# New order of TensorE units, new list priorities and new planner durations in a segment-recurrent attention kernel

## The chip, the cores and the metric

The kernel runs on one core of one Trainium2 chip. The metric is the time of one execution on the device in microseconds (us).

## The reference

`A` is a transformer layer with a recurrent memory, `B` a GELU feed-forward network; each has a layernorm ahead of it, and B normalizes once more inside. With 2048 tokens, width 512, 32 heads of 128, 8 memory rows, segments of 32 tokens and a hidden width of 1792:

```
mem = mem0
for s in range(64):
    h = concat([mem, x[32*s : 32*s+32]])            # 8 + 32 rows
    q, k, v = h @ Wq, h @ Wk, h @ Wv                # 32 heads of 128
    p = softmax(where(mask, q @ k.T / sqrt(128), -1e9))
    o = (p @ v) @ Wo
    mem = o[:8]                                     # next segment's memory
    outs.append(o[8:])
h  = x + A(layernorm(x))
h2 = h + B(layernorm(h))     # B(x) = gelu(layernorm(x) @ w1 + b1) @ w2 + b2
```

The segments depend on one another through `mem`: the next segment's projections need this segment's output projection.

## The kernel before, in words

All weights are loaded once into SBUF. For every segment TensorE runs units, most of them four matmuls side by side in the four column groups of the array:

- K0, K1, Q0, Q1, V0, V1: projections of the first and second 16 heads, four passes each (one per 128 rows of the width). `passes` (L796, and L547 where the stationary operand of the unit before is kept) records them. A pass is four matmuls of 512 columns.
- SC0, SC1 (`sc_mm`, L963): scores of the memory rows and of the 8 last tokens; `sc_softmax` follows with a max on VectorE (`nmc`, L972), the exponentials on ScalarE (`EC`, L976), a reciprocal (`rsc`, L979), a product (`PC`, L982) and a transpose (`PTC`, L983) on VectorE.
- PV0, PV1 (`pv_c`, L994 and L998): the product of those probabilities with V. SA (`sa_mm`, L1025) are the scores of the other 24 tokens' rows, whose result no later segment needs; PVA (`pv_a`, L1055, two units) is their product with V, done one segment later. PV and PVA use 32 rows of the array and all its columns (MR in the code); the other units of the loop use all rows and 32 columns (MC).
- WO (`wo_units`, L1083, eight units): the output projection. Then VectorE transposes (`TT`, L1095) and sums halves into `hT` (L1089), the next segment's memory rows.
- F0, F1: work that does not belong to the recurrence. For segments 4b to 4b+2 it is the K, Q or V projection of the last 8 tokens of each of the next four segments (`hB`, eight passes); for segment 4b+3 it is eight passes of `wo_B` (FB, L1112), all counted as F1.

`place(s)` names segments 1 to 3 a1 to a3, 60 to 63 z60 to z63 and the 56 between them m0 to m3 by s mod 4. `ORDERS[place]` is TensorE's order in a segment, written out: "V1.0.2" takes units 0 and 1 of V1. `TURNED[place]` lists the projections whose passes run backwards. Everything on the other engines is placed by a list scheduler (`Sched.schedule`) when the program is built:

```
heapq.heappush(heap, (-o.rank - BONUS.get(o.key, BONUS.get(o.kind, 0.0)), pos[o], o.gidx, o))
```

`rank` is the longest path of planned durations to the end, `BONUS` adds a number in us per kind of result and place (`PTC0@m3`: the PTC of SC0 in a segment of place m3). An operation taken from the heap goes into the first free gap of its engine on the planner's clock, and copies out of PSUM go to VectorE or ScalarE, whichever ends sooner. Each engine's instructions then run in the order of their planned starts, with semaphore waits; engines run their queues in order. The durations (`dur=`), `SWITCH` (a change between MC and MR) and `HOP` (the way from engine to engine) exist only in the planner.

Layernorm of later tokens (`ln1`, L734 to L738) runs in places m1 and later: statistics on VectorE, `rst` with a power on GpSimd (L737), then `xn` on VectorE. `nat` does the same for the attention's output (L1134 to L1137). After segment 63 comes the feed-forward network, whose order on TensorE is fixed in the code, as is `START`, the order of segment 0.

## Time and profile before

| | us |
|---|---|
| median of 3 executions | 805.24 |
| lowest, highest | 804.34, 806.07 |
| profiled execution: span from the first to the last instruction | 802.2 |

The page gives the profiled execution as its span alone; its own time is among those of the first two rows, some 3 us above the span. In the rows of the profile the columns are the start in us from the start of the span, the length in us, engine, line, operation, result and operands, shape and count; a bracket tells the idle time before and what ended it. The rows for TensorE begin where a matmul begins to read, and their ends overlap the next one's start, so the cost of a unit is read from its start to the next start.

### The profile page before, as it was taken

Reading aid. Unit: us, or ns where it says so; the run is one execution under the profiler, and the core shown is the slowest. Engines: PE = TensorE matmul, PEld = TensorE weight load, DVE = VectorE, ACT = ScalarE, POOL = GpSimd, SP = SyncE. Lnnn points to the kernel's source line nnn. Section 1 sums busy time; section 2 is a strip of 40 time slices with the busy share of each in tenths; the row PEclk is TensorE's granted clock in tenths of the full one; section 3 lists DMA queues with packets and bytes.
Section 4 is the critical chain, followed back from the end, with each engine's and each line's share of the span. In section 5 each row is a group of like instructions: output and inputs, shape, how many; then the busy total and the mean of one; then the engine's idle time right before and its main releaser. Section 6 shows DMA issues by size and latency. Waiting matters only on the chain.

```text
span 802.2 us, 46835 instructions
## 1 busy us (share of the span) xinstructions
PE 775.9 (97%) x21699; PEld 423.1 (53%) x20880; DVE 600.7 (75%) x1847; ACT 558.0 (70%) x1580; POOL 90.1 (11%) x211
## 2 busy tenths in 40 slices
...
DMA packets 65555, 48.77 MB, mean 61 GB/s; under 512 B 28996, under 2 KB 63308, under 8 KB 63820
## 3 DMA queue, kind: packets, MB, share of 16 engines
...
q8 instruction: 166, 2.72, 1.4%
q14 instruction: 33, 0.27, 0.1%
q10 hardware_dynamic: 332, 0.27, 0.1%
...
## 4 chain that ended last, share of the span: by engine, by line
PE 91%; DMA 3%; DVE 2%; ACT 1%; SPq 1%; issue 1%; POOL 0%; DVEq 0%; ACTq 0%
PE ps L796 43%; PE ps L1083 15%; PE ps L547 8%; PE quad L1465 6%; PE ps L1451 5%; DMA WQ<-in_A_Wq_dram 3%; PE ps L1112 3%; PE quad L994 3%; PE quad L1055 2%; PE ps L1025 2%; PE ps L1233 1%; PE ps L963 1%; PE quad L963 1%; SPq L708 1%; PE quad L998 1%
## 5 line engine op out<-in xcount | busy, mean ns | idle before, releaser
L1083 PE MATMUL ps<-WO,OT 128*32 128x256 bf16 x4224 | 140.6, 274 | 0.1
L796 PE MATMUL ps<-WQ,hT 128*32 128x512 bf16 x1864 | 131.6, 379 | 0.7 <-DVE hT L1089 0.5
L796 PE MATMUL ps<-WV,hT 128*32 128x512 bf16 x1364 | 125.2, 381 | 0.0
L796 PE MATMUL ps<-WK,hT 128*32 128x512 bf16 x1700 | 123.6, 380 | 0.1
L815 ACT ACTIVATE kq<-ps 128x512 bf16<-128x512 f32 x160 | 95.4, 597 | 32.3 <-PE ps L796 26.4
L1083 PEld LDWEIGHTS ps<-WO,OT 128*32 128x32 bf16 x4224 | 100.9, 96 | 26.5 <-ACT OT L814 5.5
L814 ACT CAST kq<-ps 128x512 bf16<-128x512 f32 x162 | 94.8, 585 | 19.9 <-PE ps L796 13.1
L814 ACT CAST OT<-quad 128x128 bf16<-128x128 f32 x191 | 84.4, 442 | 27.0 <-PE quad L998 18.8
L839 DVE STREAM_TRANSPOSE KALL<-kq 128x256 f32<-128x256 f32 x160 | 71.2, 445 | 15.0 <-ACT kq L814 11.8
L796 PEld LDWEIGHTS ps<-WQ,hT 128*32 128x32 bf16 x1864 | 50.3, 97 | 58.8 <-issue 19.0
L861 POOL COPY ZC<-QTB 128x256 bf16<-128x256 bf16 x64 | 25.6, 401 | 477.2 <-PE ps L963 455.7
L796 PEld LDWEIGHTS ps<-WK,hT 128*32 128x32 bf16 x1700 | 45.8, 96 | 56.9 <-issue 14.5
L547 PE MATMUL ps<-WV,hT 128*32 128x512 bf16 x684 | 67.6, 379 | 0.0
L796 PEld LDWEIGHTS ps<-WV,hT 128*32 128x32 bf16 x1364 | 38.4, 97 | 47.3 <-issue 36.6
L839 DVE STREAM_TRANSPOSE QT<-kq 128x256 f32<-128x256 f32 x128 | 57.0, 445 | 6.5 <-ACT kq L815 1.9
L1454 ACT ACTIVATE WQ<-ps,b1t 128x512 bf16<-128x512 f32 x42 | 28.9, 688 | 46.6 <-PE ps L1451 46.6
L1095 DVE STREAM_TRANSPOSE TT<-ps 128x256 f32<-128x256 f32 x66 | 29.7, 450 | 36.3 <-PE ps L1083 36.1
L814 ACT CAST VS<-ps 128x512 bf16<-128x512 f32 x65 | 38.1, 586 | 26.6 <-PE ps L796 26.5
L814 DVE CAST VS<-ps 128x512 bf16<-128x512 f32 x63 | 41.8, 663 | 5.4 <-PE ps L796 5.4
L1541 DVE TENSOR_TENSOR WV<-quad,WV 128x512 bf16<-128x512 f32 (+1 forms) x16 | 10.5, 672 | 45.6 <-PE quad L1465 45.6
L982 DVE TENSOR_TENSOR PC<-EC,rsc 128x128 bf16<-128x128 f32 x128 | 39.7, 310 | 4.3
L1112 PE MATMUL ps<-WO,OTB 128*32 128x512 bf16 x512 | 42.1, 381 | 0.4 <-issue 0.2
...
## 6 DMA issues: line engine op xcount, KB each, us to landing
...
```

What stands on the lines that cost most here:

```text
L547: return e.add_instruction(mybir.InstMatmult(name="I-%d" % (4000000 + _kept[0]), engine=mybir.EngineType.PE, start_tensor_calc=start, stop ...
L796: ins = e.matmul(o, l, m, start=(k == 0), stop=(k == DC - 1), tile_position=(0, 32 * j), skip_group_check=True)
L814: return {"act": (lambda e: e.copy(out, src), t_act(n, ps_)), "dve": (lambda e: e.tensor_copy(out, src), 0.16 + 1.042e-3 * n * fast)}
L815: return {"act": (lambda e: e.mul(out, src, scale_), t_act(n, ps_)), "dve": (lambda e: e.tensor_scalar(out, src, scale_, None, ALU.mult), ...
L839: S.op("dve", lambda e: e.transpose(out, src), reads=[("kq", i)], writes=[key], dur=t_dve(256) + 0.02, after=after)
L982: S.op("dve", lambda e: e.tensor_tensor(PC[:, r].rearrange("p t a -> p a t"), EC[:, r], bc, ALU.mult), reads=[("EC", r), ("rsc", r)], writ ...
L1083: ins = e.matmul(ps[bank][32 * j:32 * j + 32, 0:256], lhs(slot(h)), wo_cols(h, b), start=(k == 0), stop=(k == 15), tile_position=(0, 32 * ...
L1095: S.op("dve", lambda e: e.transpose(tt.rearrange("p c q t -> p (c q t)"), ps[bank][:, 0:256]), reads=[("ps", bank)], writes=[("TT", par)], ...
L1112: ins = e.matmul(ps[bank][32 * j:32 * j + 32, :], OTB[:, bk % 2, slot(h), :], WO[:, h, :], start=(k == 0), stop=(k == 7), tile_position=(0 ...
L1451: ins = e.matmul(ps[bank][:, 0:SBT], W1[:, cc, fc * P:(fc + 1) * P], hnT_of(k)[:, cc, :], start=(cc == 0), stop=(cc == DC - 1))
L1454: S.op("act", lambda e: e.activation(gT[:, fc, :], ps[bank][:, 0:SBT], ACTF.Gelu_apprx_tanh, bias=b1t[:, fc:fc + 1], scale=1.0), reads=[(" ...
L1465: S.op("pe", lambda e: e.matmul(quad[:, t, :], lhs, W2[:, fc, :], **flags), reads=[("W2", part_of(fc))] + gT_keys(k, fc), writes=[("ps", t ...
```

## The change

Only numbers and strings of the plan change, and one operand pair on GpSimd. `ORDERS` and `TURNED` are new for all eleven places. `BONUS` is new as a whole (several hundred entries; the lines with the entries that the prediction names are shown). `SWITCH` and the planned durations of five kinds of TensorE units change. In `nat` the sum var + 1e-5 becomes var * 1.00001 + 1e-10, in the same instruction. No unit, copy, transfer or buffer is added or removed.

```diff
--- before.py
+++ after.py
-SWITCH = 0.1
+SWITCH = 0.095
...
-         "PTC0@m0": -40, "PTC0@m1": 0, "PTC0@m2": 40, "PTC0@m3": -6.68, "PTC0@z60": 10.07, "PTC0@z61": -2.97, "PTC0@z62": 0.85, "PTC0@z63": 2.87,
...
-         "nmc1@a1": 40, "nmc1@a2": 0, "nmc1@a3": -8.5, "nmc1@m0": 5.59, "nmc1@m1": 10.8, "nmc1@m2": 0, "nmc1@m3": 0, "nmc1@z60": 0,
...
-         "rsc0@m0": -40, "rsc0@m1": -40, "rsc0@m2": -8.83, "rsc0@m3": -40, "rsc0@z60": -10.97, "rsc0@z61": 0.08, "rsc0@z62": -13.33,
...
-         "sma@z63": 5.36, "st": 4.55, "st@a1": -40, "st@a2": 9.73, "st@m1": 1.68, "st2": 7.35, "st2@m0": -5.76, "st2@z60": -3.49, "vd@m2": 3.83,
...
+         "PTC0@m0": 38.35, "PTC0@m1": 43.59, "PTC0@m2": -56.34, "PTC0@m3": 39.21, "PTC0@z60": -37.64, "PTC0@z61": -43.05, "PTC0@z62": -3.43,
...
+         "nmc0@z61": 30.27, "nmc0@z62": -37.98, "nmc0@z63": 0, "nmc1": 1.64, "nmc1@a1": 40, "nmc1@a2": -36.64, "nmc1@a3": 3.86, "nmc1@m0": 34.96,
+         "nmc1@m1": 40, "nmc1@m2": -36.44, "nmc1@m3": -36.44, "nmc1@z60": 46.32, "nmc1@z61": 3.56, "nmc1@z62": -40, "nmc1@z63": -36.44,
...
+         "rsc0@a3": 40, "rsc0@m0": -98.2, "rsc0@m1": -39.55, "rsc0@m2": 31.11, "rsc0@m3": -40, "rsc0@z60": 42.35, "rsc0@z61": -40, "rsc0@z62": -40,
...
+         "sma@z63": -6.26, "st": -43.67, "st2": 38.55, "st2@m0": 39.47, "st2@z60": -6.12, "st@a1": -35.8, "st@a2": -40.62, "st@m1": -35.98,
...
-TURNED = {"a1": "K0 Q1 V0", "a2": "K0 Q0", "a3": "V1", "m0": "F0 F1 Q0 V0", "m1": "K0 K1 Q1 V0", "m2": "F0 K0 K1 V0", "m3": "F1 K0 K1 Q1 V0", "z60": "F1 K0 K1 V0 V1", "z61": "Q0 Q1 V0", "z62": "F1 K0 Q0", "z63": "K0 K1 V0 V1"}
-ORDERS = {"a1": "Q0.0.3 K1.0.1 Q0.3.4 K0.0.2 Q1.0.1 K0.2.4 Q1.1.4 K1.1.4 SC0.0.2 V0.0.3 V1.0.1 V0.3.4 V1.1.2 SC1.0.1 V1.2.4 PVA.0.2 PV0.0.1 F1.0.1 WO.0.2 PV1.0.1 WO.2.8 F1.1.2 SA.0.1 F1.2.4",
-          "a2": "K0.0.1 Q0.0.4 K0.1.4 Q1.0.4 K1.0.4 SC0.0.1 V0.0.4 V1.0.3 SC1.0.1 V1.3.4 PVA.0.2 PV0.0.1 F1.0.2 WO.0.2 PV1.0.1 WO.2.8 SA.0.1 F1.2.4",
-          "a3": "Q0.0.2 K0.0.2 Q0.2.4 K0.2.4 Q1.0.4 K1.0.4 SC0.0.1 V0.0.1 V1.0.1 V0.1.4 V1.1.2 SC1.0.1 PVA.0.2 V1.2.4 PV0.0.1 F1.0.2 WO.0.2 PV1.0.1 WO.2.8 F1.2.4 SA.0.1",
-          "m0": "Q0.0.2 Q1.0.1 Q0.2.4 K0.0.4 Q1.1.4 K1.0.4 SC0.0.1 V0.0.1 V1.0.2 V0.1.2 V1.2.3 V0.2.4 SC1.0.1 V1.3.4 F0.0.1 PVA.0.2 PV0.0.1 F0.1.4 WO.0.2 PV1.0.1 WO.2.8 F1.0.4 SA.0.1",
-          "m1": "K0.0.1 Q0.0.2 K0.1.2 Q0.2.4 K0.2.3 Q1.0.1 K0.3.4 Q1.1.4 K1.0.4 SC0.0.1 V1.0.1 V0.0.2 V1.1.2 V0.2.3 V1.2.3 V0.3.4 SC1.0.1 V1.3.4 F0.0.1 PVA.0.2 PV0.0.1 F0.1.4 WO.0.2 PV1.0.1 WO.2.8 F1.0.3 SA.0.1 F1.3.4",
-          "m2": "K0.0.2 Q0.0.4 K0.2.4 Q1.0.4 K1.0.4 SC0.0.1 V1.0.1 V0.0.2 V1.1.2 V0.2.3 V1.2.3 V0.3.4 SC1.0.1 V1.3.4 F0.0.2 PVA.0.2 PV0.0.1 F0.2.4 WO.0.2 PV1.0.1 WO.2.8 SA.0.1 F1.0.4",
-          "m3": "K0.0.1 Q0.0.2 K0.1.2 Q0.2.4 K0.2.4 Q1.0.4 K1.0.4 SC0.0.1 V1.0.1 V0.0.1 V1.1.2 V0.1.3 V1.2.3 V0.3.4 SC1.0.1 F1.0.1 V1.3.4 PVA.0.2 PV0.0.1 F1.1.5 WO.0.1 PV1.0.1 WO.1.8 F1.5.7 SA.0.1 F1.7.8",
-          "z60": "Q0.0.3 Q1.0.1 Q0.3.4 Q1.1.2 K0.0.4 Q1.2.4 K1.0.4 SC0.0.1 V1.0.1 V0.0.4 V1.1.2 SC1.0.1 V1.2.4 PVA.0.2 PV0.0.1 F0.0.4 WO.0.2 PV1.0.1 WO.2.8 SA.0.1 F1.0.4",
-          "z61": "K0.0.1 Q0.0.4 K0.1.4 Q1.0.4 K1.0.4 SC0.0.1 V0.0.4 V1.0.3 SC1.0.1 V1.3.4 PVA.0.2 PV0.0.1 F0.0.4 WO.0.2 PV1.0.1 WO.2.8 F1.0.4 SA.0.1",
-          "z62": "K0.0.1 Q0.0.4 K0.1.4 Q1.0.4 K1.0.4 SC0.0.1 V0.0.2 V1.0.1 V0.2.4 V1.1.3 SC1.0.1 V1.3.4 PVA.0.2 PV0.0.1 F0.0.4 WO.0.2 PV1.0.1 WO.2.8 SA.0.1 F1.0.4",
-          "z63": "Q0.0.2 K0.0.1 Q0.2.4 K0.1.4 Q1.0.4 K1.0.4 SC0.0.1 V0.0.4 V1.0.3 SC1.0.1 V1.3.4 PVA.0.2 PV0.0.1 F1.0.4 WO.0.2 PV1.0.1 WO.2.4 F1.4.5 WO.4.7 F1.5.6 WO.7.8 F1.6.8 SA.0.1"}
+TURNED = {"a1": "K1 Q0", "a2": "K0 K1 Q0 V0", "a3": "Q1 V1", "m0": "Q0 Q1 V0", "m1": "F0 F1 K0 K1 Q1 V0 V1", "m2": "K1 Q0 V0", "m3": "K0 K1 Q1 V1", "z60": "K0 K1 Q1 V0 V1", "z61": "K0 Q0 Q1", "z62": "K0 K1 Q0 Q1 V0", "z63": "K0 Q0 V1"}
+ORDERS = {"a1": "SC0.0.1 Q0.0.1 K0.0.2 Q0.1.2 K0.2.3 Q0.2.4 K0.3.4 Q1.0.1 K1.0.1 Q1.1.4 K1.1.4 V1.0.1 SC0.1.2 V0.0.2 V1.1.2 V0.2.4 SC1.0.1 PVA.0.1 V1.2.4 PVA.1.2 PV0.0.1 WO.0.2 PV1.0.1 WO.2.8 F1.0.1 SA.0.1 F1.1.4",
+          "a2": "K0.0.1 Q0.0.4 K0.1.4 Q1.0.4 K1.0.4 SC0.0.1 V0.0.1 V1.0.2 V0.1.4 SC1.0.1 V1.2.4 PVA.0.2 PV0.0.1 WO.0.2 PV1.0.1 WO.2.8 F1.0.2 SA.0.1 F1.2.4",
+          "a3": "Q0.0.1 K0.0.1 Q0.1.4 K0.1.4 Q1.0.4 K1.0.4 SC0.0.1 V1.0.2 V0.0.4 SC1.0.1 V1.2.4 PVA.0.2 PV0.0.1 F1.0.1 WO.0.2 PV1.0.1 WO.2.8 F1.1.4 SA.0.1",
+          "m0": "Q0.0.2 Q1.0.1 Q0.2.3 K0.0.1 Q0.3.4 K0.1.4 Q1.1.3 K1.0.1 Q1.3.4 K1.1.4 SC0.0.1 V1.0.1 V0.0.1 V1.1.2 V0.1.3 V1.2.3 V0.3.4 SC1.0.1 F0.0.1 V1.3.4 PVA.0.2 PV0.0.1 F0.1.4 WO.0.2 PV1.0.1 WO.2.8 F1.0.2 SA.0.1 F1.2.4",
+          "m1": "K0.0.1 Q0.0.1 K0.1.2 Q0.1.2 Q1.0.1 Q0.2.4 K0.2.3 K1.0.1 K0.3.4 Q1.1.2 K1.1.2 Q1.2.4 V1.0.1 K1.2.4 SC0.0.1 V1.1.2 V0.0.4 V1.2.3 SC1.0.1 PVA.0.2 V1.3.4 F0.0.2 PV0.0.1 F0.2.4 WO.0.2 PV1.0.1 WO.2.8 SA.0.1 F1.0.4",
+          "m2": "Q0.0.1 K0.0.1 Q0.1.4 K0.1.4 Q1.0.4 K1.0.4 SC0.0.1 V0.0.1 V1.0.1 V0.1.2 V1.1.2 V0.2.3 V1.2.3 V0.3.4 SC1.0.1 F0.0.1 V1.3.4 PVA.0.2 PV0.0.1 F0.1.4 WO.0.2 PV1.0.1 WO.2.8 SA.0.1 F1.0.4",
+          "m3": "Q0.0.1 K0.0.2 Q0.1.2 K0.2.3 Q0.2.4 K0.3.4 Q1.0.3 K1.0.1 Q1.3.4 K1.1.4 SC0.0.1 V1.0.1 V0.0.2 V1.1.2 V0.2.4 V1.2.3 SC1.0.1 V1.3.4 PVA.0.2 PV0.0.1 F1.0.4 WO.0.2 PV1.0.1 WO.2.8 F1.4.6 SA.0.1 F1.6.8",
+          "z60": "Q0.0.4 K0.0.1 Q1.0.1 K0.1.4 Q1.1.2 K1.0.1 Q1.2.4 K1.1.4 SC0.0.1 V1.0.1 V0.0.2 V1.1.2 V0.2.4 V1.2.4 SC1.0.1 F0.0.2 PVA.0.2 PV0.0.1 F0.2.4 WO.0.2 PV1.0.1 WO.2.8 SA.0.1 F1.0.4",
+          "z61": "Q0.0.1 K0.0.4 Q0.1.4 Q1.0.4 K1.0.4 V0.0.1 SC0.0.1 V1.0.1 V0.1.4 V1.1.2 SC1.0.1 V1.2.4 F0.0.1 PVA.0.2 PV0.0.1 F0.1.4 PV1.0.1 WO.0.8 F1.0.4 SA.0.1",
+          "z62": "Q0.0.3 Q1.0.1 K0.0.1 Q0.3.4 K0.1.4 K1.0.1 Q1.1.4 K1.1.4 SC0.0.1 V1.0.2 V0.0.1 V1.2.3 V0.1.3 SC1.0.1 V0.3.4 V1.3.4 PVA.0.1 F0.0.2 PVA.1.2 PV0.0.1 F0.2.4 WO.0.2 PV1.0.1 WO.2.8 SA.0.1 F1.0.4",
+          "z63": "Q0.0.2 K0.0.1 Q0.2.4 K0.1.4 Q1.0.2 K1.0.1 Q1.2.4 K1.1.2 SC0.0.1 K1.2.4 V1.0.1 V0.0.1 V1.1.2 V0.1.3 V1.2.3 V0.3.4 V1.3.4 PVA.0.1 SC1.0.1 PVA.1.2 PV0.0.1 F1.0.2 SA.0.1 F1.2.3 WO.0.3 PV1.0.1 F1.3.4 WO.3.8 F1.4.8"}
...
-                         dur=0.215 * len(parts), mode=MC, ni=4 + 4 * len(parts))
+                         dur=0.2165 * len(parts), mode=MC, ni=4 + 4 * len(parts))
...
-                 writes=[bkey], dur=0.13, mode=MC, ni=32)
+                 writes=[bkey], dur=0.12, mode=MC, ni=32)
...
-            S.op("pe", f, reads=[("VS", s % 3, r), ("PTC", r)] + [("VBD", bk % 2, j) for j in range(4)], writes=QK, dur=0.16, mode=MR, ni=40)
+            S.op("pe", f, reads=[("VS", s % 3, r), ("PTC", r)] + [("VBD", bk % 2, j) for j in range(4)], writes=QK, dur=0.145, mode=MR, ni=40)
...
-            S.op("pe", f, reads=[("QT", 0), ("QT", 1), ("KA", par, 0), ("KA", par, 1)], writes=[("ps", bank)], dur=0.25, mode=MC, ni=64)
+            S.op("pe", f, reads=[("QT", 0), ("QT", 1), ("KA", par, 0), ("KA", par, 1)], writes=[("ps", bank)], dur=0.235, mode=MC, ni=64)
...
-                S.op("pe", f, reads=[("VS", par, half), ("PTA", s % 2)], writes=QK, dur=0.13, mode=MR, ni=32)
+                S.op("pe", f, reads=[("VS", par, half), ("PTA", s % 2)], writes=QK, dur=0.108, mode=MR, ni=32)
...
-            S.op("pool", lambda e: e.tensor_scalar(rs, ag[:, 1:2], 1e-5, None, ALU.add), reads=[("ag2", bk)], writes=[("rs2", bk)], dur=0.2)
+            S.op("pool", lambda e: e.tensor_scalar(rs, ag[:, 1:2], 1.00001, 1e-10, ALU.mult, ALU.add), reads=[("ag2", bk)], writes=[("rs2", bk)], dur=0.2)

```

4 lines of the change are left out of this document (2 added, 2 removed), and 131 rows, old and new, of the table BONUS.

## The prediction

> **What bounds the kernel now.** I read the page first, then the stretch of the segment loop, then TensorE's rows in order of time, and last VectorE's rows at the two places where TensorE waits. From the page (span; busy share of TensorE; chain that ended last, by engine; the queue that carries instructions):
>
> ```profile
> span 802.2 us, 46835 instructions
> ...
> PE 775.9 (97%) x21699; PEld 423.1 (53%) x20880; DVE 600.7 (75%) x1847; ACT 558.0 (70%) x1580; POOL 90.1 (11%) x211
> ...
> q8 instruction: 166, 2.72, 1.4%
> ...
> PE 91%; DMA 3%; DVE 2%; ACT 1%; SPq 1%; issue 1%; POOL 0%; DVEq 0%; ACTq 0%
> ```
>
> TensorE holds 91% of the chain, so only its own order and what it waits for can move the time. The loop, with busy time of PE, PEld, DVE, ACT and POOL, the clock and the DMA share:
>
> ```profile
> 80.00:658.00 578.00, 576.63 (x18329) 319.84 (x17354) 496.94 (x1565) 442.89 (x1314) 47.07 (x119) 1.00 0.14 31
> ```
>
> The clock is full. "Busy" counts overlapping ends, so waits have to be read from starts. First passes of segments 1, 4, 60 and 63, then of 27, 29, 30 and 31:
>
> ```profile
> 49.03 1.02 PE L796 MATMUL ps<-WQ,hT 128*32 128x512 bf16 x12
> ...
> 79.91 0.83 PE L796 MATMUL ps<-WQ,hT 128*32 128x512 bf16 x12 [0.24 <-DVE hT L1089]
> ...
> 658.85 0.83 PE L796 MATMUL ps<-WQ,hT 128*32 128x512 bf16 x12
> ...
> 690.38 0.62 PE L796 MATMUL ps<-WQ,hT 128*32 128x512 bf16 x8
> ```
>
> ```profile
> 318.44 0.40 PE L796 MATMUL ps<-WK,hT 128*32 128x512 bf16 x4
> ...
> 339.16 0.40 PE L796 MATMUL ps<-WK,hT 128*32 128x512 bf16 x4
> ...
> 349.38 0.61 PE L796 MATMUL ps<-WK,hT 128*32 128x512 bf16 x8
> ...
> 359.61 0.40 PE L796 MATMUL ps<-WK,hT 128*32 128x512 bf16 x4
> ```
>
> Segments 4 to 59 are 56 segments, 14 of each place, in 658.85 - 79.91 = 578.94 us. The inside of segment 27 (place m3), from its first score unit to the next segment's first pass, with two rows of segment 28 behind it:
>
> ```profile
> 321.90 0.30 PE L963 MATMUL quad<-KALL,ZC 128*32 128x64 bf16 x16
> ...
> 323.53 0.31 PE L963 MATMUL ps<-KALL,ZC 128*32 128x64 bf16 x16
> 323.65 0.40 PE L1112 MATMUL ps<-WO,OTB 128*32 128x512 bf16 x4
> ...
> 324.20 0.37 PE L1055 MATMUL quad<-PTA,VS 32*128 32x32 bf16 x32
> 324.49 0.27 PE L994 MATMUL quad<-PTC,VS 32*128 32x16 bf16 x16
> ...
> 324.73 1.05 PE L1112 MATMUL ps<-WO,OTB 128*32 128x512 bf16 x16
> 325.60 0.39 PE L1083 MATMUL ps<-WO,OT 128*32 128x256 bf16 x8
> 325.93 0.27 PE L994 MATMUL quad<-PTC,VS 32*128 32x16 bf16 x16
> ...
> 326.17 1.71 PE L1083 MATMUL ps<-WO,OT 128*32 128x256 bf16 x56
> 327.70 0.60 PE L1112 MATMUL ps<-WO,OTB 128*32 128x512 bf16 x8
> 328.14 0.40 PE L1025 MATMUL ps<-KALL,QT 128*32 128x32 bf16 x32
> 328.36 0.41 PE L1112 MATMUL ps<-WO,OTB 128*32 128x512 bf16 x4
> 328.86 1.26 PE L796 MATMUL ps<-WQ,hT 128*32 128x512 bf16 x20
> 329.95 1.04 PE L796 MATMUL ps<-WK,hT 128*32 128x512 bf16 x16
> 330.81 0.82 PE L796 MATMUL ps<-WQ,hT 128*32 128x512 bf16 x12
> ```
>
> Prices from start to start: a pass (329.95 to 330.81, four of them) 0.215; a WO unit (326.17 to 327.70, seven) 0.219; a score unit 0.12; SA 0.22. So segment 27 took 328.86 - 318.44 = 10.42, segment 28 (m0) 10.30, segment 29 (m1) 10.22, segment 30 (m2) 10.23: 41.17 for a clean group of four, 576.4 for 14 groups. The other 2.5 us of the 578.94 are single stalls. Two waits recur. At the tail, FB at 328.36 should last 0.22 and lasts 0.50: TensorE waits 0.28 for the next memory rows. In the middle, PVA to PV0 takes 0.29. VectorE there, and the one large stall:
>
> ```profile
> 323.91 0.29 DVE L972 TENSOR_REDUCE nmc<-ps 128x2 f32<-128x128 f32 x1
> 324.12 0.23 DVE L983 STREAM_TRANSPOSE PTC<-PC 128x64 f32<-128x64 f32 x1
> ...
> 327.56 0.41 DVE L738 TENSOR_SCALAR xn<-xr,agg,rst 128x512 bf16<-128x512 bf16 x1 [1.00 <-POOL rst L737]
> 327.93 0.45 DVE L1095 STREAM_TRANSPOSE TT<-ps 128x256 f32<-128x256 f32 x1
> ```
>
> ```profile
> 159.12 0.19 PE L1055 MATMUL quad<-PTA,VS 32*128 32x32 bf16 x2 [0.67 <-issue]
> ```
>
> **The change, part by part.** The work is the same; counting the order strings gives the same units for every place. The sum is made against the span of 802.2 us; the median of the runs is 805.24, so 3.0 us lie around the span and I leave them.
>
> m3, tail. WO's end at 327.70 to the next segment's start takes 1.16, a fixed chain (TT, the sum, hT). Now 3 FB passes and SA (0.87) cover it; the new order puts 4 FB passes and SA (1.08) there, so 0.21 of wait goes: -0.21 x 14 = -2.9. The pass comes from between SC1 and PVA, so the stretch SC0 to PV0, now 324.49 - 321.90 = 2.59, falls to 2.38 if nothing waits. SC1 to PV1 keeps 2.40 (an FB pass replaced by a WO unit). PV0 waits for PTC, and VectorE runs PTC behind the second score unit's max: swapped, PTC would end 0.21 sooner, which is just enough. The new bonuses set PTC0@m3 from -6.68 to 39.21 and nmc1@m3 from 0 to -36.44, which asks for the swap, but rsc0@m3, two steps ahead of PTC0, stays at -40, level with nmc1. Without the swap PV0 waits 0.21 and the whole gain is gone. I take half: -1.5, ends -2.9 and 0.
>
> m1, one more trip into row tiling. The new order puts a V pass and two F0 passes between PVA and PV0, so the array changes shape six times in place of four. Into row tiling costs 0.11 (325.60 to 325.93 is 0.33 against 0.22). The way out is seen once, in segment 3, which has such a trip, beside a PVA that did not wait (segment 26):
>
> ```profile
> 74.78 0.37 PE L1055 MATMUL quad<-PTA,VS 32*128 32x32 bf16 x32
> 75.08 0.61 PE L796 MATMUL ps<-WV,hT 128*32 128x512 bf16 x8
> ```
>
> ```profile
> 314.19 0.37 PE L1055 MATMUL quad<-PTA,VS 32*128 32x32 bf16 x32
> 314.40 0.30 PE L994 MATMUL quad<-PTC,VS 32*128 32x16 bf16 x16
> ```
>
> PVA then leaves after 0.30 against 0.21, so a trip is 0.20. The wait of 0.08 ahead of PV0 goes with it: +0.12 x 14 = +1.7. Ends: +2.8, if PV0 had not really been waiting, and 0, if VectorE sets m1's length and TensorE only waits less. The page on the chip says the same with no price: the Trainium skill, TensorEngine Tiling (Array Packing), Key Properties, has it that changing the tiling mode drains TensorE. The trace agrees; by that rule alone m1 pays the full +2.8 and the time is 1.1 above my sum, which is counted in rival C too.
>
> m0, tail. SA was last; the new order puts two F1 passes behind it, as m1 had before. Those two places had the same counts and differed by 0.08: -0.07 x 14 = -1.0, ends -1.1 and +1.0.
>
> m2. One F0 pass moves from ahead of PVA to behind PV0, so SC0 to PV0 becomes the 2.59 of m3 with its small wait; the group shows what that costs: +0.03 x 14 = +0.4, ends 0 and +1.0.
>
> Single stalls, 2.5 us. The one at 159.12 waits for no semaphore, in a stream of 16 KB instruction blocks (2.72 MB in 166). A new order moves every block edge. Half of them gone: -1.3; ends -2.5 and +2.5. A page of the Trainium skill, Runtime: NRT & Kernel Launch, section Instruction fetch mechanics, says that crossing such a block is mostly hidden; that one row of 0.67 stands among 166 blocks agrees with mostly. By that rule this term is 0 and the sum 1.3 higher, which is counted in rival C.
>
> Segments 1 to 3 take 79.91 - 49.03 = 30.88 though they lack most F work, so they run on latency. SC1 comes a pass earlier in a2 (0.21), a3 loses a trip (0.20), a1 gains one that its waits cover and has its mask unit moved ahead of the projections, for which I put a pass (0.21): -0.6, ends -0.9 and +0.4. Segments 60 to 62 take 690.38 - 658.85 = 31.53, 0.84 above three clean ones of 10.23; z60 and z61 are evened out, z62 and z63 gain a trip each (+0.4): -0.2, ends -0.8 and +0.8.
>
> One answer, nothing: TURNED only flips the direction of passes whose price is 0.215 either way; SWITCH and the durations feed the planner alone; the second POOL operand sits in the same 16 instructions on an engine 11% busy, read by the FFN long after. START, the FFN's order and the weight queue stay; their evacuations are re-sorted: 0, ends -1 and +1.
>
> Sum: -1.5 + 1.7 - 1.0 + 0.4 - 1.3 - 0.6 - 0.2 = -2.5. Span 799.7, time 802.7.
>
> **Rivals.** B, a larger gain: the swap holds, m1's trip is covered by VectorE's pace, most single stalls go: -2.9 + 0 - 1.0 + 0 - 2.5 - 0.9 - 0.4 = -7.7, 797.5. For it: VectorE is busy 497 of 578 us in the loop, so it can be the one that sets m1. Against it: every term must come out at its good end.
>
> C, the change does not do what it says: PTC0 stays behind nmc1, m1 pays the full trip, stalls only move: 0 + 2.8 - 1.0 + 0.4 + 0 - 0.6 - 0.2 = +1.4, and half of the stalls' term back brings it to about 0: 805.2. For it: -40 on rsc0@m3, and a trip is a shown cost.
>
> D, slower: VectorE's queue runs in order, and at 327.56 it sat 1.00 on POOL's power for xn, then ended just as TT (the head of the tail's chain) could start. The bonus of that statistic, st@m1, falls from 1.68 to -35.98. If the wait slides 0.5 later, TT and the next segment slide with it, once in each of 14 groups: +7.0, 809.7. It decides from 0.3 on (+4.2 against a forecast of -2.5). Against it: xn is needed segments later, so it may slide far past TT and cost nothing.
>
> **How the numbers follow.** 0.2% (1.6 us) is about what a measurement of this kernel can tell from no change. My forecast 802.7 has 0.40, with a range of its own of 800.5 to 805.0: 0.30 of it faster, 0.10 the same. B has 0.20, all faster. C has 0.18: 0.14 the same, 0.04 slower. D has 0.22, all slower. So faster 0.50, same 0.24, slower 0.26. The range 797 to 810 leaves out about half of B below and half of D above, 0.2 together; the ends of single terms, added on one side, would go further than that, to 796 and 815.
>
> **What would show it.** Right: m3 segments near 10.3, with 4 FB passes and SA behind WO and 0.07 of wait; PTC ahead of nmc in m3; PVA to V at 0.30 in m1 and m1 segments near 10.35; m0 near 10.23. Wrong: PVA to PV0 at 0.5 in m3 (no swap); VectorE idle on POOL rst with TT behind it and more than 1.16 from WO's end to the next segment; new rows ended by issue; the first passes of segment 1 or the FFN off by over 1 us, which my sum leaves at 0.

## The result, and the profile after

| us | before | after |
|---|---|---|
| median of 4 executions in the same rounds | 805.65 | 816.61 |
| lowest, highest | 804.34, 806.22 | 814.44, 816.99 |
| profiled execution: time | | 814.44 |
| profiled execution: span | 802.2 | 812.7 |

The changed kernel takes 1.0123 times as long, 95% interval 1.010 to 1.0145. The forecast was 802.7, its range 797 to 810: it is slower, and outside the range. The page of the changed kernel, in the same lines as before:

```profile
span 812.7 us, 46821 instructions
...
PE 782.4 (96%) x21699; PEld 419.0 (52%) x20761; DVE 581.7 (72%) x1789; ACT 576.6 (71%) x1638; POOL 87.3 (11%) x211
...
q8 instruction: 166, 2.72, 1.4%
...
PE 93%; DMA 3%; DVE 1%; SPq 1%; ACT 1%; issue 1%; DVEq 0%
```

TensorE has the same 21699 matmuls. VectorE has 58 instructions fewer (1847 to 1789) and ScalarE 58 more (1580 to 1638): copies out of PSUM have changed engine. The prediction had no term for that in the loop. First passes of segments 4 and 60 after:

```profile
81.27 1.05 PE L796 MATMUL ps<-WQ,hT 128*32 128x512 bf16 x16
...
668.69 0.84 PE L796 MATMUL ps<-WQ,hT 128*32 128x512 bf16 x12
```

Segments 4 to 59 take 587.42 instead of 578.94: +8.5 of the 10.5 us. From the other first passes (segment 1 at 50.89, segment 63 at 700.45): the start +1.9, segments 1 to 3 -0.5, segments 60 to 62 +0.2, the rest +0.4. By place, from first pass to first pass, 14 segments each:

| us | before: median, mean | after: median, mean |
|---|---|---|
| m0 | 10.295, 10.299 | 10.290, 10.659 |
| m1 | 10.251, 10.293 | 10.478, 10.525 |
| m2 | 10.221, 10.222 | 10.303, 10.303 |
| m3 | 10.425, 10.539 | 10.409, 10.471 |

The medians give -0.1, +3.2, +1.1 and -0.2, in sum +4.0; what single segments lie above them was 2.2 us before (the prediction, from a clean group, had 2.5) and is 6.7 after. The waits of TensorE between 80 and 690 us (engine, tile, line, what was waited for: total us, times, longest), first before, then after:

```profile
PE quad L1055 <- issue: 0.7, 1, 0.7
PE ps L796 <- DVE hT L1089: 0.2, 1, 0.2
PE ps L1112 <- issue: 0.2, 1, 0.2
```

```profile
PE quad L994 <- DVE PTC L983: 3.1, 1, 3.1
PE quad L994 <- issue: 1.7, 2, 1.0
PE ps L1112 <- issue: 0.8, 3, 0.5
```

So there are three causes: one wait of 3.1 us for a PTC, stalls for instructions (2.5 us in place of 0.9), and a longer median in m1 and m2. The long wait is in segment 52 (m0). The rows of VectorE and PE there, in order of time:

```profile
587.34 0.37 DVE L1224 TENSOR_SCALAR xn<-xT,agg,rst 128x512 bf16<-128x512 bf16 x1
587.63 0.16 DVE L979 RECIPROCAL rsc<-smc 128x2 f32<-128x2 f32 x1
...
589.60 0.24 DVE L983 STREAM_TRANSPOSE PTC<-PC 128x64 f32<-128x64 f32 x1
...
590.39 0.68 DVE L1120 TENSOR_TENSOR oBn<-OTB 32x512 bf16<-32x512 f32 x1
591.10 0.30 DVE L982 TENSOR_TENSOR PC<-EC,rsc 128x128 bf16<-128x128 f32 x1
591.44 0.24 DVE L983 STREAM_TRANSPOSE PTC<-PC 128x64 f32<-128x64 f32 x1
591.74 0.26 PE L994 MATMUL quad<-PTC,VS 32*128 32x16 bf16 x16 [3.08 <-DVE PTC L983]
```

The reciprocal for SC0 is there at 587.63, behind an `xn` of the feed-forward network's layernorm. The planner then put the product and transpose that PV0 needs behind those of SC1 (589.60) and behind `oBn`: 591.44. VectorE is idle for 0.21 us only in this stretch (ahead of the second max, at 588.00); it does other work first. The `xn` puts the reciprocal 0.33 us later than it could be, and on the planner's clock the product for PV0 then no longer fits into the gap ahead of the second max, so the plan has it behind all the others. That is how 0.3 us becomes a wait of 3.1.

### The profile page after: what moved, and what is told of

Its sections match the earlier page's. It is cut to its first block, busy times and chain, and to the rows that moved or that the text cites. A ratio compares the mean times of both kernels' runs of the same rounds, so it can differ in the third digit from the quotient of the medians.

```text
span 812.7 us, 46821 instructions
## 1 busy us (share of the span) xinstructions
PE 782.4 (96%) x21699; PEld 419.0 (52%) x20761; DVE 581.7 (72%) x1789; ACT 576.6 (71%) x1638; POOL 87.3 (11%) x211
## 4 chain that ended last, share of the span: by engine, by line
PE 93%; DMA 3%; DVE 1%; SPq 1%; ACT 1%; issue 1%; DVEq 0%
PE ps L796 43%; PE ps L1083 15%; PE ps L547 8%; PE quad L1465 6%; PE ps L1451 5%; PE ps L1112 4%; DMA WQ<-in_A_Wq_dram 3%; PE quad L994 3%; PE quad L1055 2%; PE ps L1025 2%; PE ps L1233 2%; PE ps L963 2%; PE quad L963 1%; SPq L708 1%; PE quad L998 1%
## 5 line engine op out<-in xcount | busy, mean ns | idle before, releaser
L796 PE MATMUL ps<-WK,hT 128*32 128x512 bf16 x1868 | 143.5, 380 | 0.0
L796 PE MATMUL ps<-WV,hT 128*32 128x512 bf16 x1496 | 125.3, 379 | 0.0
L796 PE MATMUL ps<-WQ,hT 128*32 128x512 bf16 x1584 | 125.1, 385 | 0.2
L814 ACT CAST OT<-quad 128x128 bf16<-128x128 f32 (+1 forms) x192 | 85.2, 444 | 30.5 <-PE quad L998 24.1
L796 PEld LDWEIGHTS ps<-WK,hT 128*32 128x32 bf16 x1868 | 52.7, 97 | 64.4 <-issue 13.8
L796 PEld LDWEIGHTS ps<-WQ,hT 128*32 128x32 bf16 x1584 | 43.4, 97 | 66.5 <-issue 23.4
L796 PEld LDWEIGHTS ps<-WV,hT 128*32 128x32 bf16 x1496 | 43.4, 96 | 40.3 <-issue 23.5
L839 DVE STREAM_TRANSPOSE QT<-kq 128x256 f32<-128x256 f32 x128 | 55.2, 431 | 7.8 <-ACT kq L815 3.1
L547 PE MATMUL ps<-WV,hT 128*32 128x512 bf16 x552 | 55.2, 379 | 0.0
L814 ACT CAST VS<-ps 128x512 bf16<-128x512 f32 x79 | 46.3, 586 | 9.6 <-PE ps L796 8.9
L547 PE MATMUL ps<-WQ,hT 128*32 128x512 bf16 x464 | 46.0, 379 | 0.0
L976 ACT ACTIVATE EC<-ps,nmc 128x64 f32<-128x64 f32 x130 | 39.7, 310 | 4.1 <-DVE nmc L972 3.7
```

The costliest lines, as they stand in the source:

```text
L547: return e.add_instruction(mybir.InstMatmult(name="I-%d" % (4000000 + _kept[0]), engine=mybir.EngineType.PE, start_tensor_calc=start, stop ...
L796: ins = e.matmul(o, l, m, start=(k == 0), stop=(k == DC - 1), tile_position=(0, 32 * j), skip_group_check=True)
L814: return {"act": (lambda e: e.copy(out, src), t_act(n, ps_)), "dve": (lambda e: e.tensor_copy(out, src), 0.16 + 1.042e-3 * n * fast)}
L839: S.op("dve", lambda e: e.transpose(out, src), reads=[("kq", i)], writes=[key], dur=t_dve(256) + 0.02, after=after)
L976: ins = e.activation(EC[:, r, sl, :], o[:, 64 * sl:64 * sl + 64], ACTF.Exp, bias=nmc[:, r, sl:sl + 1], accum_out=smc[:, r, sl:sl + 1])
```

## The experiments

Ratios are to the kernel before, run on the same chip. LOCK is a constant of the kernel that pads TensorE's stream with empty instructions at the third unit of each m0, so that a block of 256 instructions ends at a chosen place; both kernels had 106:

```
if LOCK is not None and o.tag is not None and units == SKIP + 1 and seg % 4 == 0 and seg:
    owed = (LOCK - at) % FETCH_N
```

"Margin" is the last number in the rule by which a TensorE unit with several semaphore waits hands the earlier ones to units ahead of it:

```
if c.start < p.start + p.dur + self.lat(p, o) + 0.1:
    break
```

**1. Segment 52's `xn` (r_hn).** The changed kernel, with `hn0`, the early `xn` of L1224, given a lower priority in m0.

```diff
+BONUS = {"hn0@m0": -40, ...
```

> One priority is added to the changed kernel: the next block's early normalisation in segment 52 (hn0@m0) goes behind the softmax statistics rsc0 of the same segment in VectorE's queue. Theory (one place, one loss): segment 52 falls from 13.53 to the 10.3 of its neighbours, the wait of 3.08 us ahead of PV0 is gone, nothing else moves; span 812.7 - 3.2 = 809.5, ratio to the kernel before 1.0123 - 0.0040 = 1.008. Rival (the displaced normalisation hurts where it lands): the stall reappears in segment 53 or 54, as a wait on VectorE or on hT, and the span stays within 1 us of 812.7, ratio 1.011 to 1.013.

812.19 us, 1.007 [1.0051, 1.0089], as the theory had it. In segment 52 PTC for PV0 now runs at 590.53 and PV0 at 590.89 without a wait; the `xn` that stood ahead of the reciprocal now runs behind both PTCs, at 593.89. Half a per cent of the 1.23 is this one priority: 4.4 us by the medians, more than the wait of 3.1 (experiment 5 shows why). The profiled execution does not show the gain, since at 815.56 it is the longest of its six. Segment 52 does not fall to the expected 10.3 but takes 11.21, because PV1 stalls for instructions:

```profile
590.53 0.23 DVE L983 STREAM_TRANSPOSE PTC<-PC 128x64 f32<-128x64 f32 x1
...
590.89 0.27 PE L994 MATMUL quad<-PTC,VS 32*128 32x16 bf16 x16
...
593.21 0.25 PE L994 MATMUL quad<-PTC,VS 32*128 32x16 bf16 x13 [0.69 <-issue]
```

**2. The opening (r_warm).** After the change TensorE waits twice for Wq near 33 us, and the granted clock halves. Row of a matmul with its wait, then windows (window, length, busy time of PE, PEld, DVE, ACT, POOL, clock, DMA share, GB/s) of the changed kernel:

```profile
35.34 0.62 PE L796 MATMUL ps<-WQ,hB 128*32 128x512 bf16 x4 [2.12 <-DMA WQ<-in_A_Wq_dram]
```

```profile
35.00:37.00 2.00, 1.66 (x16) 0.61 (x20) 0.30 (x1) 0.60 (x1) 0.00 (x0) 0.50 1.10 349
```

Filler passes go into the order of segment 0:

```diff
-         ("B", "Q", 0, (0, 5)), "Q0", ...
+         ("W", 7, 20), ("B", "Q", 0, (0, 5)), "Q0", ...
```

> 20 filler passes (results unused) are put into the opening of the changed kernel, where TensorE sits for the pieces of WQ at 30.8 and 33.2 us. Theory (the idle time itself costs the clock): the granted clock stays at 1.00 from 33 to 41 us, the 12 passes behind the last WQ piece take 0.215 each in place of 0.42, and segment 1 starts near 48.9, 2.0 us earlier than 50.89; ratio 1.010. Rival (the clock falls at that time whatever TensorE did, or the opening's end is set by the scalar and vector work): segment 1 still starts at 50.5 to 50.9, ratio 1.012.

818.47 us, 1.0151 [1.0129, 1.0173]. The clock did stay at 1.00 from 35 to 39, but the fillers moved the block edges, and a stall of 1.82 for instructions came at 46.04, after which the clock halved (windows and row of this kernel):

```profile
35.00:37.00 2.00, 1.62 (x36) 0.68 (x32) 0.19 (x1) 0.61 (x2) 0.00 (x0) 1.00 1.10 352
...
47.00:49.00 2.00, 2.00 (x40) 1.45 (x36) 0.45 (x1) 0.60 (x1) 0.00 (x0) 0.50 0.69 205
```

```profile
46.04 1.47 PE L796 MATMUL ps<-WQ,hB 128*32 128x512 bf16 x11 [1.82 <-issue]
```

A miss as a repair. Twelve profiles have the changed opening without the fillers. In all of them TensorE waits twice for Wq (1.7 to 2.3 us each), and the clock is halved behind it. Segment 1 begins between 49.33 and 49.80 where that lasts 3.4 us, and between 49.99 and 51.14 where it lasts 6.8, as in the changed kernel's profile. In the seven profiles with the old opening (one wait for Wq, of 1.0 to 1.9) it begins between 48.84 and 49.20. So the change's opening does cost something, 0.1 to 2.3 us, and the start's +1.9 is one of the longer ones.

**3. The trip in m1 (r_m1).** The changed kernel with PVA directly ahead of PV0 in m1.

```diff
-"... SC1.0.1 PVA.0.2 V1.3.4 F0.0.2 PV0.0.1 ..."   "EC1@m1": 40
+"... SC1.0.1 V1.3.4 F0.0.2 PVA.0.2 PV0.0.1 ..."   "EC1@m1": -40
```

> In the place m1 of the changed kernel the memory-row unit PVA is put directly ahead of PV0, so that one of the two trips into row tiling goes (one priority, EC1@m1, follows, with no other effect planned). Theory (a trip costs its own 0.2 and nothing covers it): m1 falls from 10.48 to 10.25, 14 x 0.23 = 3.2 us, span 809.5, ratio 1.008. Rival (VectorE sets the pace in m1, and the trip lay in time that PV0 would have waited anyway, as the planner has it): m1 stays at 10.45 to 10.53, PV0 waits 0.2 or more for PTC, span 812 to 814, ratio 1.012 or above.

814.17 us, 1.0096 [1.0078, 1.0115]; m1's median goes from 10.478 to 10.461 only, as the rival had it, and the ratio lies between the two expectations. By medians of the 14 segments, 0.32 us went with the trip (0.20, and a wait of 0.11 ahead of PVA, where after the change PVA waits for two engines), and 0.19 came back as a wait ahead of PV0 and 0.11 ahead of PV1. Segment 29 in this kernel:

```profile
346.14 1.07 ACT L814 CAST VS<-ps 128x512 bf16<-128x512 f32 x2
...
346.42 0.29 DVE L972 TENSOR_REDUCE nmc<-ps 128x2 f32<-128x128 f32 x1
...
347.10 0.33 ACT L976 ACTIVATE EC<-ps,nmc 128x64 f32<-128x64 f32 x1
...
348.39 0.24 DVE L983 STREAM_TRANSPOSE PTC<-PC 128x64 f32<-128x64 f32 x1
...
348.69 0.26 PE L994 MATMUL quad<-PTC,VS 32*128 32x16 bf16 x16
```

The max of SC1 ends at 346.71, but ScalarE is busy with two VS copies until 347.1, and PV1 starts as soon as its PTC ends. One of these copies was VectorE's before. Segment 29 as a window, before and then after:

```profile
339.16:349.38 10.22, 10.22 (x332) 5.38 (x301) 9.05 (x29) 8.03 (x25) 0.40 (x1) 1.00 0.06 19
```

```profile
341.97:352.45 10.48, 10.45 (x333) 5.68 (x313) 8.79 (x29) 8.71 (x26) 1.14 (x3) 1.00 0.07 20
```

VectorE loses 0.26 and ScalarE gains 0.68. Over the 14 segments of m1 the summed rows of both grow by some 1.1 us a segment (18.9 to 20.0), in segments of 10.2 to 10.5.

**4. The copy in m1 alone (r_b_vs).** The kernel before, with VS of the second half in m1 forced onto ScalarE (`FORCE` limits the planner's choice of engine).

```diff
+FORCE = {'VS1@m1': 'act'}
...
+                if o.alts and FORCE.get(o.key, eng) != eng:
+                    continue
```

> The kernel before, with another part of the change added: in m1 the second value copy (VS) and the prefill for the memory rows' scores go from VectorE to ScalarE, TensorE's order stays as it was. ScalarE's busy time in m1 goes from 8.84 to 9.8 of 10.2 us. Theory (ScalarE is late for the second softmax there, and PV1 waits): m1 grows by 0.1 to 0.25, +1.5 to +3.5 us in 14 segments, ratio 1.002 to 1.0045, with the added time ahead of PV0 or PV1. Rival (only the extra trip of TensorE made m1 long): m1 stays at 10.22, ratio 0.999 to 1.001.

810.43 us, 1.007 [1.0049, 1.0091]; m1's median is 10.666, more than expected. So ScalarE's load by itself can make m1 longer, but not at the place expected: of the 0.42 by which the median grows, 0.25 is the first WO unit's wait for its copy (OT) on ScalarE, and 0.15 lies in the tail, where a block ends. After the change the order is another, and this wait is not there. The way back (r_m1v) did not work: experiment 1 and the order of experiment 3, with that copy forced onto VectorE and m1's priorities searched anew.

```diff
+FORCE = {'VS1@m1': 'dve'}
```

> The changed kernel with segment 52 mended and one trip into row tiling taken out of m1 (as in the two runs before), and in m1 the second value copy and one prefill given back to VectorE, with m1's priorities chosen anew around that. ScalarE's busy time in m1 goes from 10.40 to 9.4. Theory (ScalarE set m1's length, so taking out the trip alone gave nothing): m1 falls from 10.46 to 10.25 to 10.35, 1.5 to 3 us less than the run with segment 52 mended (ratio 1.007): 1.0035 to 1.005. Rival (VectorE, 9.5 busy and now 10.5, takes over as the bound): m1 stays at 10.45 or goes up, ratio 1.007 or more.

820.25 us, 1.0189 [1.0166, 1.0213]; m1's median is 10.514, and PV1 of m0, a place that the edit does not touch, stalls for instructions in 11 of 14 segments.

**5. Block edges alone (r_lock, r_lock100).** The changed kernel with another LOCK. The order and the waits are the same; only where the blocks end differs.

```diff
-LOCK = 106
+LOCK = 22
```

> Only the position of the instruction-block edges is moved (the alignment constant 106 becomes 22), so that the edge in PV1 of m0, and those in PVA and PV1 elsewhere, fall among projection passes. Theory (the two stalls of 0.96 and 0.69 us in segments 48 and 8, which wait for no semaphore, are late instruction blocks hit by units that use up instructions fast): both vanish and no such stall takes their place, span 812.7 - 1.7 = 811.0 within 0.4, ratio 1.010. Rival (the stalls are a transfer's contention at that time, wherever the edge is): stalls without a semaphore of 0.5 us or more remain in segments 8 and 48 or appear in one or two others, span 812 to 813.5.

840.36 us, 1.0414 [1.0389, 1.044]: 24 us over the changed kernel (medians) from block edges alone, against the direction that was expected. The first two rows of TensorE's waits between 80 and 690 us:

```profile
PE ps L1112 <- issue: 3.7, 9, 0.6
PE ps L1083 <- issue: 3.1, 10, 1.2
```

By the count of the instructions 141 block edges lie in segments 4 to 59. Set against the same units of the changed kernel, TensorE is late at these edges by 22 us in sum, about what segments 4 to 59 are longer by (21.8; a part of the 22 is hidden by later waits, and segment 52 has 2.6 more from the halved clock shown below). Where TensorE uses up a block fast it mostly stalls at its end, here counted from 0.15 on: in 16 of 27 blocks from a V pass or PVA over PV to WO (2.7 to 3.0 us without the stall, where units are many short instructions; up to 1.4 us late), in 10 of 14 from F0 to F1 in m1 (2.7 to 3.1), and in all 14 that end in m3's tail (3.2; 0.25 to 0.8 late). Of 56 blocks that take over 5 us, 42 end without a delay, and the 14 that end at SC0 of m3 have about 0.15 each. In between the length does not decide: 14 blocks of 3.5 us in m3 all stall (0.2 to 0.5), and 14 of 3.3 to 3.5 in m1 never do. So the rule of 3.4 us that the next expectation reads from this run does not hold. The next block's transfer starts 0.6 to 1.6 us after the edge in eight of ten.

```diff
-LOCK = 106
+LOCK = 100
```

> The changed kernel with the alignment constant at 100 in place of 106. From the run with 22 I read a rule: an instruction block is there about 3.4 us after the edge ahead of it was crossed, and TensorE stalls where a block is used up in less. With 106 the shortest blocks of the loop last 3.47 and 3.58 us, with 100 3.63 us. Theory (the rule holds and the scattered stalls in PV1 of m0 and the tail of m3 are the short blocks with a late transfer): these stalls shrink from 4.4 us in all to 1 to 3 us, ratio 1.008 to 1.011. Rival (106 is as good as 100, the stalls depend on something else than the block's length): ratio 1.0115 to 1.0145.

815.13 us, 1.0121 [1.01, 1.0142], in the range of the rival. The small stalls are some 2 us less in the profile, and segment 52 hides it: it takes 16.13 instead of 13.53. Its wait for PTC is 3.1 as before, but behind it the clock is halved. The window behind the wait, here and then in the changed kernel's profile:

```profile
587.20:590.00 2.80, 2.76 (x68) 1.36 (x68) 0.34 (x2) 0.85 (x2) 0.00 (x0) 0.50 0.06 15
```

```profile
591.70:594.00 2.30, 2.26 (x89) 1.50 (x93) 0.51 (x2) 1.26 (x4) 0.00 (x0) 1.00 0.07 19
```

Of the five profiles that have this wait (the changed kernel's, r_warm, r_m1, r_lock, r_lock100), four show the halved clock, and segment 52 is 16.1 to 16.2 in them; the changed kernel's own does not, and it is the fastest of its four executions. So segment 52 costs 5.9 us in most of them.

**6. The copy for SC1 (r_b_zc), and the wait that comes with it (r_b_zc_w1).** After the change a pass ahead of SC1 lasts longer in m0, m2 and m3 (0.28 to 0.33 instead of 0.216), and the copy ZCm1 that SC1 reads is on ScalarE there. The kernel before with only that:

```diff
+FORCE = {'ZCm1@m0': 'act', 'ZCm1@m1': 'act', 'ZCm1@m2': 'act', 'ZCm1@m3': 'act'}
```

> The kernel before, with one thing of the change added: the copy of the second score unit's queries (ZC, second half) is made by ScalarE in place of VectorE in all four places, as the changed kernel has it (the queues are planned anew around it; in m3 one value copy follows to ScalarE). Theory (the copy stands behind the exponentials in ScalarE's queue, so the second score unit waits): the pass ahead of SC1 lasts 0.05 to 0.12 longer in m0, m2 and m3 as it does in the changed kernel, the segments grow by about 0.05 to 0.1 each, +3 to +5 us over 56 segments, ratio 1.004 to 1.006. Rival (that wait only moves one that came later, ahead of PV0 or in the tail): segments within 0.02 of before, ratio 0.999 to 1.002.

836.98 us, 1.0381 [1.0347, 1.0415]. The pass ahead of SC1 became 0.328 to 0.331 as expected, but 0.115 x 56 is 6.4 us and not 31. SC1 now waits for two engines (ScalarE for the query copy, VectorE for the keys), as SC0 did in m2 already, and PV1 of m2 stalls for instructions in all 14 segments (0.8 to 1.4 us). The second kernel moves second waits to earlier units and leaves the copy on ScalarE; of 135 units with two waits in the loop, 14 are left, none a score unit:

```diff
-                    if c.start < p.start + p.dur + self.lat(p, o) + 0.1:
+                    if c.start < p.start + p.dur + self.lat(p, o) + -0.1:
```

> The kernel before with the query copy of the second score unit on ScalarE (it came out at 1.038), and one number more: a second semaphore wait of a TensorE unit is moved to an earlier unit even where the planner sees it fulfilled only 0.1 us after that unit's start (before: not unless 0.1 us ahead of it). No score unit then carries two waits. Theory (two waits at both score units delay the fetch of the next block): the stall of about 1 us in PV1 of m2, in all of its segments, goes, and m2 falls from 11.35 to 10.3 or 10.4; 15 to 20 us less, ratio 1.012 to 1.02, with the 0.11 ahead of SC1 kept. Rival (the waits only stand beside it): m2 stays above 11, ratio 1.03 or more.

805.63 us, 0.9994 [0.9984, 1.0005]. One number took all 31 us back, more than expected. TensorE's waits between 80 and 690 us, of the first and of the second kernel (two of five rows, and both):

```profile
PE quad L997 <- issue: 16.1, 18, 1.3
PE quad L1058 <- issue: 2.5, 6, 0.5
```

```profile
PE ps L799 <- DVE hT L1092: 0.3, 1, 0.3
PE ps L799 <- issue: 0.2, 1, 0.2
```

Segment 10 (m2) in both shows how. These kernels' lines are three further on (L966 is the score unit, L997 PV). The first kernel: the last pass ahead of SC1 and SC1; PV1, broken in two; and the DMA engines' busy share in 40 slices of 0.1 us from 149.9:

```profile
150.88 0.40 PE L799 MATMUL ps<-WV,hT 128*32 128x512 bf16 x4
151.22 0.30 PE L966 MATMUL ps<-KALL,ZC 128*32 128x64 bf16 x16
...
153.62 0.21 PE L997 MATMUL quad<-PTC,VS 32*128 32x16 bf16 x7
154.49 0.23 PE L997 MATMUL quad<-PTC,VS 32*128 32x16 bf16 x9 [0.66 <-issue]
```

```profile
DMA  0000000000000000000000600000000000000000
```

The second kernel, the same rows, and the slices from 145.9:

```profile
146.97 0.39 PE L799 MATMUL ps<-WV,hT 128*32 128x512 bf16 x4
147.21 0.30 PE L966 MATMUL ps<-KALL,ZC 128*32 128x64 bf16 x16
...
149.61 0.27 PE L997 MATMUL quad<-PTC,VS 32*128 32x16 bf16 x16
```

```profile
DMA  0080000000000000000000000000000000000000
```

By the count of the instructions, a block ends in V0 at 149.96 in the first and at 146.23 in the second. The instruction block that moves next lands 2.1 us after that edge in the first (the digit at 152.1) and at the edge in the second (146.1). The next edge is in PV1, 3.66 us on, and there TensorE waits only in the first. The pass ahead of SC1 takes 0.34 and 0.24: about 0.09 goes with the double wait there, and 0.02 is left for the later copy. This is no price of every double wait: SC0 of m2 has one in the kernel before, and the pass ahead of it takes 0.216 all the same.

Over 19 profiles (all but r_lock) I counted the m0 and m2 segments in which a block ends in V0 or V1, by the waits in the kernels' plans. Where both score units carry two waits, PV1 is over 0.3 us late in 51 of 72; where at most one does, in 1 of 460. The changed waits also shift the edges (in segment 10 from the third instruction of V0 to the fifth), so the edge's place is a rival. It does not explain this: where the edge cuts the V pass after 5 or 6 of its 8 instructions, PV1 is late in 31 of 46 with two waits at both score units, and in none of 190 otherwise. In all 52 late cases the next block's transfer started over 2 us after the edge; in the other 480 it did so in 3 only. The changed kernel has four segments of the first kind, all in m0, and its two stalls at PV1 are two of these (segments 8 and 48). In the loop 79 units carried two waits before, and 170 after.

**7. Other edges for the repaired orders.** Experiment 1 with LOCK 105 and 102, the kernel before with 103, and r_m1v with 105, each with this line alone:

```diff
-LOCK = 106
+LOCK = 102
```

> The same with 102, which makes the shortest block of the loop longest by my reckoning (3.62 us; 3.47 with 106). Theory (the block's length is what counts, beside the one bad position): few stalls in m3's tail and none in m0, ratio 1.002 to 1.005. Rival (another position is as bad as 5 of 8 was): a stall of about 1 us in every segment of one place, ratio 1.015 or more.

> The changed kernel with segment 52 mended (1.007), and the alignment constant 105 in place of 106, which moves every edge of the loop one instruction later. Theory: segments 8, 48, 52 and 56, where PV1 still stalled by 0.9 to 1.5 us, fall to 10.3; 2 to 4 us less, ratio 1.002 to 1.005. Rival (the later edge makes other blocks short, in the tail of m3 above all, and the time comes back there): ratio 1.006 or more.

> The kernel before with the alignment constant 103 in place of 106, so that its block from PVA of m1 to the tail lasts 3.3 us in place of 3.25 and its other short ones 3.5 or more. Theory (its single stalls, 2.5 us in all, are short blocks): 0.5 to 1.5 us less, ratio 0.998 to 1.000. Rival (106 is already the good place, another has a bad position in it): ratio 1.004 or more, with a stall of about 1 us that comes back in every fourth segment.

> The run with VS and the prefill of m1 back on VectorE, which came out at 1.0189, with one number changed: the alignment constant goes from 106 to 105, so that every instruction-block edge of the loop comes one instruction later. In all traces so far, PV1 of m0 stalls by 0.9 to 1.4 us in most segments where the edge in the V pass behind SC0 cuts that pass after 5 of its 8 instructions, and in none where it cuts it after 6; that run had 5 of 8 in 13 of its 14 m0 segments. Theory (this one instruction is where its 11 us went): the stalls in PV1 of m0 are gone, m0 falls from 11.43 to 10.3, span 820.4 to about 809, ratio 1.004 to 1.007. Rival (the stalls belong to that run's order of work and only move): ratio 1.014 or more.

Measured: r_hn102 808.78, 1.0025 [1.0006, 1.0045]; r_hn105 811.15, 1.0048 [1.0029, 1.0068]; r_b103 806.27, 0.9996 [0.998, 1.0012]; r_m1v105 816.01, 1.012 [1.0085, 1.0154]. The first three lie in the range of their theory, the last between its two. Edges alone give the changed order up to 0.45%, and the old order nothing. In the last kernel the stalls of m0 stay in 10 segments with the edge one matmul further on, so the edge's exact place in the pass is not what decides.

**8. The waits moved further (margin -0.3).** r_m1v, and r_hn102, with

```diff
-                    if c.start < p.start + p.dur + self.lat(p, o) + 0.1:
+                    if c.start < p.start + p.dur + self.lat(p, o) + -0.3:
```

> The run with VS and the prefill of m1 on VectorE (1.0189; 1.012 with the constant 105), with second waits moved to earlier units up to 0.3 us ahead of their planned fulfilment; no score unit carries two. The edge in m0 cuts the V pass at 6 of 8, where the run with 105 still stalled in 10 of 13 segments. Theory: no stall in PV1 of m0, which falls to 10.25 to 10.35; ratio 1.003 to 1.007. Rival: m0 stays near 11.2, ratio 1.012 or more.

> The changed kernel with segment 52 mended and the constant 102 (1.0025), with second waits moved in the same way. Theory: the last stall in PV1 of m0 goes, and with the edges of m3 now in PV0 and SA some of the stalls in m3's tail; 0.5 to 2.5 us less, ratio 0.9995 to 1.002. Rival (an earlier wait costs up to 0.2 in each segment where it is not yet fulfilled): ratio 1.004 or more.

811.7, 1.0071 [1.0054, 1.0088], and 811.64, 1.0071 [1.0053, 1.0088]. The stalls of m0 are gone in the first, which has the edges of m0 at the same cut as r_m1v105 (late in 10 of 13 there, in none of 13 here), so it is the waits and not the cut. But waits that come too early now block passes themselves (0.45 for a V pass in m0, 0.47 for a K pass in m3, instead of 0.216). For r_hn102 that is a loss.

**9. The old and the new order, both with moved waits.** The kernel before with margin -0.1 (r_b_w1) and with LOCK 98 too (r_b98_w1); the changed kernel with experiment 1, margin -0.1 and LOCK 104 (r_hn104_w1).

> The kernel before with second waits moved in the same way (65 of its 79 units with two waits in the loop lose one). Theory: the single stall of segment 11 goes, the rest stays: 0 to 1.5 us less, ratio 0.998 to 1.000. Rival (earlier waits cost, or an edge lands badly): ratio 1.002 or more.

> The changed kernel with segment 52 mended, second waits moved to earlier units up to 0.1 us ahead of their planned fulfilment, and the alignment constant 104. No segment of the loop then has two waits at both score units. Theory (what is left of the change is its order of work alone): m0 10.25, m1 10.475, m2 10.275, m3 10.31 with few stalls, 41.3 us for a group of four against 41.17 in the kernel before, which has 2.5 us of stalls besides; ratio 0.999 to 1.002. Rival (moved waits cost in each segment as with 0.3 us, or stalls stay): ratio 1.005 or more.

> The kernel before with second waits moved (0.9978) and the alignment constant 98 in place of 106, which puts the edge of m1's tail behind the last F1 pass and makes that block 3.6 us long in place of 3.42. Theory (the block's length): m1 falls from 10.40 to 10.25, 1.5 to 2.5 us less, ratio 0.9945 to 0.997. Rival (a block elsewhere, V0 to PV1 of m2 with 3.25 us, now stalls in its place): ratio 0.998 or more, with PV1 of m2 longer than 0.24.

804.49, 0.9978 [0.9967, 0.999]; 804.82, 0.9987 [0.9973, 1.0001]; and 803.36, 0.9975 [0.9964, 0.9987]. The last is the fastest version found and beats both kernels, but not by the edges: m1's median did fall to 10.28, yet the ratio is that of r_b_w1 within the noise, where 0.9945 to 0.997 was expected. Its span, and its only wait of TensorE between 70 and 690 us:

```profile
span 801.6 us, 46825 instructions
```

```profile
PE ps L796 <- DVE hT L1089: 0.6, 2, 0.3
```

So from 1.0123, one priority takes the changed kernel to 1.007, and moved waits with other edges to 0.9987. With the same treatment the old order is at 0.9978 or 0.9975. r_hn104_w1 and r_b98_w1 ran in the same rounds, 12 executions each, and their means are 804.98 and 803.46: with these edges the old order is 1.5 us (0.2%) faster, clear of the noise of 0.3. So the new order by itself is worth nothing, and rather costs a little.

## Why the prediction was wrong, by its own steps

| term, us | forecast (ends) | measured |
|---|---|---|
| m3 tail | -1.5 (-2.9, 0) | -0.2 |
| m1 trip | +1.7 (0, +2.8) | +3.2 |
| m0 tail | -1.0 (-1.1, +1.0) | -0.1 |
| m2 | +0.4 (0, +1.0) | +1.1 |
| single stalls | -1.3 (-2.5, +2.5) | +4.5 |
| segments 1 to 3 | -0.6 (-0.9, +0.4) | -0.5 |
| segments 60 to 62 | -0.2 (-0.8, +0.8) | +0.2 |
| start, feed-forward network | 0 (-1, +1) | +2.3 |

The places are 14 times the difference of the medians, the single stalls what the means lie above them. The step that failed is **"single stalls"**: "half of them gone" was a guess that a new order scatters the same few stalls anew, and 3.2 of the 4.5 (5.9 where the clock halves behind it) is segment 52, whose wait was no such stall at all. The reason given, "a new order moves every block edge", was right, and r_lock shows that it can cost far more than the end of +2.5. What it left out is that the new plan changes which units wait for two engines, and that this can decide whether an edge stalls (r_b_zc against r_b_zc_w1, 31 us). This step is 5.8 of the 13.0 us between the sum and the result; the start has 2.3, m1 1.5, m3 1.3, and the other terms less than one each. The rule of the Trainium skill, Runtime: NRT & Kernel Launch, section Instruction fetch mechanics, that crossing a block is mostly hidden, holds for both kernels of this case (five stalls on 166 blocks after) and not for r_lock and r_b_zc.

**The loop's copies that change engine** have no term at all. "Their evacuations are re-sorted: 0" speaks of `START` and the feed-forward network only; for the loop the sum takes it as nothing without saying so. The planner gave 58 instructions to ScalarE. That made the double waits at SC1, and in m1 the load on ScalarE. m3, m0 and m2 show it as a pass ahead of SC1 that takes 0.33, 0.28 and 0.33 instead of 0.22.

**m3**: the mechanism held. The tail's wait is gone and PV0 follows PVA closely, and in VectorE's rows the PTC of SC0 (326.81) runs ahead of the max of SC1 (326.98): the swap took place. Segment 27 after:

```profile
326.69 0.40 PE L796 MATMUL ps<-WV,hT 128*32 128x512 bf16 x4
327.02 0.37 PE L1055 MATMUL quad<-PTA,VS 32*128 32x32 bf16 x32
327.24 0.30 PE L994 MATMUL quad<-PTC,VS 32*128 32x16 bf16 x16
...
330.94 0.46 PE L1025 MATMUL ps<-KALL,QT 128*32 128x32 bf16 x32
331.22 0.63 PE L1112 MATMUL ps<-WO,OTB 128*32 128x512 bf16 x8
331.66 1.05 PE L796 MATMUL ps<-WQ,hT 128*32 128x512 bf16 x16
```

PVA to PV0 is 0.22 (0.29 before) and the two FB passes of the tail 0.44, without a wait. This segment takes 331.66 - 321.36 = 10.30 instead of 10.42: -0.12, and 14 of these would be -1.7, close to the forecast. Eight of the 14 m3 segments give back 0.1 or more of it, some at F1, where a block ends (three waits, 0.8 us, in the view above). With waits and edges moved (r_hn104_w1) m3's median is 10.263.

**m0** moved its tail as forecast, from 1.445 to 1.373, and lost 0.06 ahead of SC1. **m2** is 10.276 with moved waits, +0.8 instead of +1.1: the forecast's +0.4 was half of it. **m1** was mis-sized. PVA's way out was 0.20, as priced, but "VectorE sets m1's length" was named as the end at which TensorE's trip costs nothing, and it is the reverse: VectorE and ScalarE together became longer, and without the trip m1 is only 0.02 shorter. The 1.5 us above the forecast are the wait ahead of PVA, which takes 0.34 from SC1 instead of 0.23, 14 times 0.11. Which of the copies or statistics would have to move back is not settled; r_m1v, which moved one, did not repair it.

**The start** lies outside its end of +1. Its mechanism, waits for Wq and the halved clock, is in the trace of this execution; the twelve profiles of experiment 2 put the change's part between 0.1 and 2.3 us, by how long the clock stays halved.

**Rival D** had the right sign and the right engine (VectorE, in order, an `xn` in the way) but the wrong place: it put the wait ahead of TT in every group, and the trace has it ahead of PV0 in one segment out of 56, six times as long. The time it gave, 809.7, falls short, since it knew nothing of the stalls. B did not come true. Of C one part did, that m1 pays the full trip (it paid 3.2, more than C's 2.8); PTC0 did not stay behind nmc1, and the time was not about the same.
